# Four early expert slots instead of two, and slot 0's first product inside the last attention batch

## The chip, the cores and the metric

The kernel runs on one core of a Trainium2 chip. The core has a matrix engine (PE, with its weight loads shown as PEld), a vector engine (DVE), a scalar engine (ACT), a general engine (POOL), and a queue engine (SP) that here only issues transfers. Each engine executes its own instructions strictly in the order in which the program gives them; semaphores hold it where it needs another's result. The metric is the device time of one execution in microseconds (us), lower is better.

## The reference

Attention over 4 batches of 8 heads, 768 positions and 64 channels, in blocks of 32 keys: every query sees its neighbours within 16 positions and one summary (maximum of k, mean of v) of each block. Its output, 3072 tokens of 512 channels, goes through a mixture of 8 experts, of which each token uses the one with the largest logit:

```python
scores_l_m = np.where(mask_l, scale * (q @ k.T), -1e9)      # |i - j| < 16
scores_s = scale * (q @ k_sum.T) + np.log(32)               # k_sum: max over 32 keys
a = softmax(concat(scores_l_m, scores_s)); x = a @ concat(v, v_sum)
e_idx = argmax(x @ w_gate); gate = softmax(x @ w_gate)[e_idx]
eom = sigmoid(x @ w_output_gate)
for e in range(8):
    out[mask_e] = gate * eom[:, e] * (relu(x[mask_e] @ w1[e]) @ w2[e])
```

w1 of an expert is 512 x 1024, w2 is 1024 x 512. All inputs and the output are float32.

## The kernel before

*Attention.* `attention` (line 169) goes through 48 stages: batch, token tile of 128 (`tok`, 6 in a batch), and half of the heads (`g`). A stage multiplies queries and keys (`scores`), takes exponentials on ACT (`pr`), transposes them on PE (`turn_p`), and multiplies by values (`values`), whose result `xs` is written to `x_dr` in DRAM. Beside that run the loads and transposes of later batches. Value blocks lie in a ring of `VR` = 9 tiles (line 34), each loaded by SP when the block that used it before is done. After every two token tiles come the logits (`turn_x`, `logits`, `turn_logits`), and after every batch the routing (`route`, line 393): the position of each token in its expert's list is counted with matmuls, and six scatters on POOL write the token numbers and factors into `l_dr`. The last batch's last logits and its routing cannot come before its last stage.

*Experts.* The tokens of an expert are worked on in slots of 256. For a slot, POOL fetches its list (`fetch_list`, line 693, two indirect transfers), gathers its tokens from `x_dr` (`fetch`, line 707, two more), PE transposes them (`take_x`, into high and low parts `xh`, `xl`), the first product makes 8 hidden blocks (`first`, line 755: 12 matmuls of 256 columns each), and the second product (`second`, line 856: 8 blocks of 6 matmuls of 512 columns) makes the output, which `write` scatters on POOL. In the middle of a slot's second product stand the transposes of the next slot's tokens and the gather for the one after it. Weights come in tiles of 128 x 512 (`fetch_w`, line 716): SP loads a raw tile, ACT makes its high part (line 733), DVE its low part (line 734). Each of w1 and w2 has 8 tiles per expert, and only one set of them is kept, so a tile is loaded when the slot before is done with it. SP reads the expert's number from the slot's table first (`value_load`).

*Slots.* `EARLY` = 2 slots are taken from what the first two batches fill: `early_slots` counts full blocks of 256 per expert after these batches' routing. Their lists and slot 0's gather are issued in the last batch (event "routed", handled by `start`). All other slots come from `rest_slots` (line 633), after the last batch's routing: as many full ones as there are, then halves of 128. Slots 1 to 7 run in any case, further ones under nested conditions.

*The hand-over.* Slot 0's w1 is loaded in the stages of token tile 3 of the last batch and the first half of its w2 in those of tile 4 (lines 782 and 783). The second half of w2 lies where attention's tiles are, so it comes after them. `early` (line 785) puts slot 0's transposes and its first product behind the last stage, with the five pieces of the last routing between its blocks (`ROUTE_AT`); then come the rest of the weights, `rest_slots`, slot 2's list, and slot 0's second product.

*Order.* A planner simulates the program and fixes each engine's order from it; within `manual_schedule` an engine keeps the order in which the program is written (SP in attention; POOL, and DVE for some weights, behind it). `late_work` lists work that the last batch's stages take along.

Of the kernel before, what the change touches and what calls it, by code (L numbers as in the profile page):

```python
# [20 lines left out]
P = 128  # L21
# [28 lines left out]
EARLY = 2  # L50
REST = N - EARLY * SLOT

SURE = -(-(REST - E * SLOT // 2) // SLOT)
MOST = (REST + E * (SLOT // 2 - 1)) // SLOT
# [39 lines left out]
def body(tc, q, k, v, w_gate, w_ogate, w1, w2, ident, cst, out):  # L94
    nc = tc.nc
    with (
# [14 lines left out]
        l_dr = dr.tile([E * N, 2], I32, name="l_dr")  # L111
# [6 lines left out]
        late_work = [[] for _ in range(TB)]  # L118
# [27 lines left out]
def route_setup(tc, const, sa, ps, c_sb, l_dr):  # L146
# [15 lines left out]
    fill = sa.tile([P, E * N // P, 2], I32, name="fill")  # L162
    nc.gpsimd.memset(fill[:, :, 1:2], 0)
    nc.gpsimd.iota(fill[:, :, 0:1], pattern=[[1, E * N // P]], base=NOLIST, channel_multiplier=E * N // P)
# [4 lines left out]
def attention(tc, const, sa, sb, st, ps, dr, q, k, v, id_sb, c_sb, wg_sb, x_dr, l_dr, rt, late_work):  # L169
# [335 lines left out]
    for i, (b, tok, g) in enumerate(stages):  # L505
        u, tt = tok // 2, tok % 2
        n1, n2 = step_after(b, u), step_after(b, u, 2)
        more = b + 1 < B
        if (b, tok, g) == (B - 1, 0, 0):
# [50 lines left out]
        if b == B - 1 and i == n - 2 * TB + 5:  # L560
            yield "routed"
# [378 lines left out]
```

## Time and profile before

| What | Value |
|---|---|
| runs | 575.73, 562.63, 572.33 us; median 572.33 |
| the profiled execution | 563.66 us, span 561.8 us, mean clock 0.949 |
| PE busy | 500.7 us, 89% of the span, 3880 matmuls |
| DVE, ACT, POOL busy | 395.9 us (70%), 339.1 us (60%), 193.1 us (34%) |
| moved by DMA | 117.63 MB, mean 209 GB/s |
| first-product matmuls | 3 lines with 384 each, that is 12 full slots |

"Busy" is the share of the span in which an engine executes; PE's matmuls overlap, so a busy PE is not PE at its peak. The clock is the share of full speed that the chip granted to PE. A wait is put down to what ended it. Attention fills roughly the first 210 us, the full slots the time to about 500 us, the halves the rest.

### The profile page before, as it was taken

To read this page: it belongs to the slowest core of one execution; us is meant where nothing else is said; L and a number is where in the kernel's file an instruction comes from. 1 tells how busy PE (TensorE), PEld (TensorE's weight loads), DVE (VectorE), ACT (ScalarE), POOL (GpSimd) and SP (SyncE) were. 2 spreads that over 40 slices of the span, in tenths; PEclk is the share of its full clock that TensorE was granted. 3 is DMA by queue.
4 is the path that set the end of the run, shared out by engine and by line. 5 is a ranking of instruction groups with operands and counts; after the bars stand their busy time and mean duration, and the time that the engine had idled before them with its cause. 6 is when DMAs were issued, how large, how long until landed. Compare 5 with 4: busy or idle time off the path is not lost. (4 is left out here: it accounts for less than half of the span.)

```text
span 561.8 us, 12246 instructions
## 1 busy us (share of the span) xinstructions
PE 500.7 (89%) x3880; PEld 436.5 (78%) x3880; DVE 395.9 (70%) x1210; ACT 339.1 (60%) x752; POOL 193.1 (34%) x222
## 2 busy tenths in 40 slices
PE   6498998988979789985999999999999999987990
PEld 5497786767768678874989989899898998975770
DVE  8878798759838857952767665776656666666892
ACT  4386786675749747442656554665555655547881
POOL 6036145445541420337643625415113031130111
PEclk8599998998979979997999999999999999998996
DMA  9979999999764874159667485774856737439790
GB/s 233 232 186 251 235 241 250 115 219 232 163 138 120 247 253 150 65 162 317 211 225 272 151 282 185 236 277 139 300 181 232 269 128 264 168 114 332 252 322 26
DMA packets 116799, 117.63 MB, mean 209 GB/s; under 512 B 53598, under 2 KB 78462, under 8 KB 115952
## 3 DMA queue, kind: packets, MB, share of 16 engines
q1 hardware_dynamic: 107584, 97.02, 61.3%
q0 software_dynamic: 9136, 19.69, 11.5%
q8 instruction: 34, 0.56, 0.5%
q14 instruction: 45, 0.37, 0.2%
HBM read 105.50 MB, written 13.79 MB: 212 GB/s over the span
## 5 line engine op out<-in xcount | busy, mean ns | idle before, releaser
L764 PE MATMUL hp<-xhl,w1h 128*128 128x256 f32 x384 | 109.0, 285 | 0.0
L765 PE MATMUL hp<-xhl,w1l 128*128 128x256 f32 x384 | 108.8, 284 | 0.0
L763 PE MATMUL hp<-xhl,w1h 128*128 128x256 f32 x384 | 108.4, 286 | 0.0
L733 ACT ACTIVATE w2h<-raw 128x512 fp32r<-128x512 f32 x104 | 64.7, 629 | 60.5 <-PE yp L854 27.7
L734 DVE TENSOR_TENSOR w2l<-raw,w2h 128x512 fp32r<-128x512 f32 x104 | 70.5, 689 | 35.2 <-ACT w2h L733 34.2
L852 PE MATMUL yp<-w2h,hh 128*128 128x512 f32 x216 | 87.3, 404 | 0.1
L853 PE MATMUL yp<-w2l,hh 128*128 128x512 f32 x216 | 85.4, 395 | 0.0
L854 PE MATMUL yp<-w2h,hl 128*128 128x512 f32 x216 | 85.2, 396 | 0.1
L331 ACT ACTIVATE pr<-sm,mn 128x120 f32<-128x120 f32 x192 | 62.1, 387 | 26.1 <-DVE mn L329 25.8
L763 PEld LDWEIGHTS hp<-xhl,w1h 128*128 128x128 f32 x384 | 73.7, 193 | 2.0 <-DVE w1l L734 0.4
L712 POOL DMA_INDIRECT xg<-x_dr,lst x28 | 32.3, 1152 | 124.5 <-PE xp L745 106.1
L764 PEld LDWEIGHTS hp<-xhl,w1h 128*128 128x128 f32 x384 | 74.1, 193 | 1.2 <-DVE xhl L748 0.2
L765 PEld LDWEIGHTS hp<-xhl,w1l 128*128 128x128 f32 x384 | 74.1, 193 | 0.0
L766 ACT ACTIVATE hh<-hp 128x256 fp32r<-128x256 f32 x96 | 36.5, 381 | 59.1 <-PE hp L765 57.0
L734 DVE TENSOR_TENSOR w1l<-raw,w1h 128x512 fp32r<-128x512 f32 x104 | 66.2, 690 | 7.3 <-ACT w1h L733 6.2
L767 DVE SCALAR_TENSOR_TENSOR hl<-hp,hh 128x256 fp32r<-128x256 f32 x96 | 39.6, 421 | 44.8 <-ACT hh L766 44.7
L321 PE MATMUL sp<-kt,qt 128*128 128x120 f32 x384 | 58.7, 301 | 7.9 <-DVE kt L296 7.0
L733 ACT ACTIVATE w1h<-raw 128x512 fp32r<-128x512 f32 x104 | 58.2, 621 | 6.9 <-DMA raw<-in_moe_w_dram 6.5
L321 PEld LDWEIGHTS sp<-kt,qt 128*128 128x128 f32 x384 | 53.8, 215 | 10.4 <-issue 8.3
L329 DVE CUSTOM_DVE_ANT_0 sm<-sp,c_sb 128x120 f32<-128x120 f32 x192 | 42.9, 277 | 14.6 <-PE sp L321 13.1
L854 PEld LDWEIGHTS yp<-w2h,hl 128*128 128x128 f32 x216 | 40.7, 189 | 9.5 <-DVE hl L823 0.5
L852 PEld LDWEIGHTS yp<-w2h,hh 128*128 128x128 f32 x216 | 41.2, 191 | 8.6 <-ACT hh L822 0.5
(285 smaller groups left out, 906.5 us busy)
## 6 DMA issues: line engine op xcount, KB each, us to landing
raw<-in_moe_w_dram SPq DMA_DIRECT2D x208, 256.0 KB
vw<-in_v_dram SPq DMA_DIRECT2D x88, 96.0 KB
raw_k<-in_k_dram SPq DMA_DIRECT2D x12, 512.0 KB
raw_q<-in_q_dram SPq DMA_DIRECT2D x12, 512.0 KB
vm<-in_v_dram SPq DMA_DIRECT2D x8, 768.0 KB
x_dr<-xs POOLq DMA_DIRECT2D x24, 256.0 KB, 5.8
vw<-vs_dr SPq DMA_DIRECT2D x36, 48.0 KB
vw<-in_v_dram SPq DMA_DIRECT2D x8, 64.0 KB
```

What stands on the lines that cost most here:

```text
L321: nc.tensor.matmul(sp[:, 2 * x + y, 0:W], lhsT=qt[:, 2 * g + x, li, :], rhs=kt[:, 2 * g + x, blk * KW:blk * KW + W], start=True, stop=True)
L329: nc.vector.tensor_tensor_reduce(out=sm[:, c, :], in0=sp[:, c, 0:W], in1=c_sb[:, m:m + W], scale=1.0, scalar=3.0e38, op0=ALU.add, op1=ALU. ...
L331: nc.scalar.activation(pr[:, c, :], sm[:, c, :], AF.Exp, bias=mn[:, c:c + 1], scale=-1.0)
L733: nc.scalar.activation(hi, raw, AF.Copy)
L734: nc.vector.tensor_tensor(lo, raw, hi.bitcast(F32), ALU.subtract)
L763: nc.tensor.matmul(hp, lhsT=w_h[:, fs], rhs=self.xh[:, c, :], start=c == 0, stop=False)
L764: nc.tensor.matmul(hp, lhsT=w_h[:, fs], rhs=self.xl[:, c, :], start=False, stop=False)
L765: nc.tensor.matmul(hp, lhsT=w_l[:, fs], rhs=self.xh[:, c, :], start=False, stop=c == NC - 1)
L767: nc.vector.scalar_tensor_tensor(hl[:, j, :], hp, 0.0, hh[:, j, :].bitcast(F32), ALU.max, ALU.subtract)
L852: nc.tensor.matmul(y, lhsT=hh[:, j, tk], rhs=w_h, start=j == 0, stop=False)
L853: nc.tensor.matmul(y, lhsT=hh[:, j, tk], rhs=w_l, start=False, stop=False)
L854: nc.tensor.matmul(y, lhsT=hl[:, j, tk], rhs=w_h, start=False, stop=j == NF - 1)
```

## The change

`EARLY` becomes 4, and the event "routed" comes in stage 10 of batch 2 (`ROUTED_AT`); the lists of all four early slots are fetched there. Their gathers read only the rows of the first two batches. At the last batch's first stage slot 0's gather is issued and `late_work` is filled from a table, `LATE`, one entry per stage: "10" is tile 0 of w1, "x" slot 0's transposes with slot 1's gather behind them, "b0" block 0 of its first product, "20" tile 0 of w2. The blocks use the PSUM tag TR. After the last stage the second half of slot 0's w2 and all of slot 1's w1 are loaded, and `tail` executes slot 0's second product in a fixed order on PE, with the five pieces of the last routing ("r" in `TAIL`) between its blocks. Then come `rest_slots` and the other slots. Their lists are fetched from slot 2 on, six per slot (three before). An early slot that does not exist would get an empty list, for which `l_dr` has 128 more rows. The ring of value tiles has 8 instead of 9.

```diff
-VR = 9
+VR = 8
+ROUTED_AT = 10
-ROUTE_AT = (-1, 0, 1, 2, 4)
+LATE = ("10 11", "12 13", "14 15", "x 16", "17 b0", "b1 20", "b2 21", "b3 22", "b4 23", "b5 b6", "b7")
+TAIL = ("r", 0, "r", 1, "r", 2, 3, "r", "r", 4, 5, 6, 7)
+LISTS = 6
-EARLY = 2
+EARLY = 4
+FIRST = 2
...
-                if event == "last batch":
+                if event == "routed":
+                    moe.add_slots(early_slots(tc, const, c_sb, rt))
+                    for s in range(EARLY):
+                        moe.fetch_list(s, 2)
+                elif event == "last batch":
                     pool_a.__exit__(None, None, None)
                     moe.open_first(tc.tile_pool(name="moe1", bufs=2, side="left", reuse_waits="tile"))
-                elif event == "routed":
-                    moe.add_slots(early_slots(tc, const, c_sb, rt))
                     moe.start(late_work)
                 elif event[0] == "tiles done":
-                    moe.early(event[1])
+                    route = event[1]
...
+        with tc.manual_schedule(engines={mybir.EngineType.DVE}):
+            moe.fetch_w(2, 0, range(NF // 2, NF))
+            moe.fetch_w(1, 1, range(NF))
+        moe.tail(route)
+        slots, halves, counts = rest_slots(tc, const, c_sb, rt)
+        moe.add_slots(slots)
+        halves = halves()
         with tc.manual_schedule(engines={mybir.EngineType.Pool}):
-            with tc.manual_schedule(engines={mybir.EngineType.DVE}):
-                moe.fetch_w(2, 0, range(NF // 2, NF))
-                moe.fetch_w(1, 1, range(NF // 2))
-                slots, halves, counts = rest_slots(tc, const, c_sb, rt)
-            moe.add_slots(slots)
-            moe.fetch_list(EARLY, 2)
-            moe.fetch_w(1, 1, range(NF // 2, NF))
-            moe.second(0, 2, *moe.hidden0, 1, 2, 2)
-            halves = halves()
             moe.run(halves)
...
+        if i == FIRST * 2 * TB + ROUTED_AT:
+            yield "routed"
...
-        if b == B - 1:
-            w = late_work[tok]
-            take = w[:-(-len(w) // 2)] if g == 0 else w[:]
-            del w[:len(take)]
-            second += take
+        if late_work:
+            second += late_work.pop(0)
...
-        rows = (B - 1) * S if s in range(EARLY) else N
+        rows = FIRST * S if s in range(EARLY) else N
...
     def start(self, late_work):
-        for s in range(EARLY):
-            self.fetch_list(s, 2)
         self.fetch(0, 2)
-        late_work[3] += [lambda: self.fetch_w(1, 0, range(NF))]
-        late_work[4] += [lambda: self.fetch_w(2, 0, range(NF // 2))]
-
-    def early(self, route):
-        self.take_x(2, "S")
-        self.fetch(1, 2)
         self.hidden0 = self.hidden()
-        for j in range(-1, NF):
-            if j >= 0:
-                self.first(j, self.hidden0, None, "S" if j % 2 else "PT")
-            if j in ROUTE_AT:
-                with self.tc.high_priority():
-                    route.pop(0)()
+        def work(what):
+            if what == "x":
+                self.take_x(2)
+                self.fetch(1, 2)
+            elif what[0] == "b":
+                self.first(int(what[1]), self.hidden0, None, "TR")
+            else:
+                self.fetch_w(int(what[0]), 0, [int(what[1])])
+        late_work += [[lambda x=x: work(x) for x in stage.split()] for stage in LATE]
+
+    def tail(self, route):
+        yp = self.accumulators(2)
+        with self.tc.manual_schedule(engines={mybir.EngineType.PE}):
+            for what in TAIL:
+                if what == "r":
+                    with self.tc.high_priority():
+                        route.pop(0)()
+                    continue
+                self.second_step(what, yp, *self.hidden0, 1, 2, 2)
+        self.write(0, yp)
...
-        later = [(s, 2) for s in range(EARLY + 1, EARLY + NITEM)] + [(("half", h), 1) for h in range(E)]
+        later = [(s, 2) for s in range(EARLY, EARLY + NITEM)] + [(("half", h), 1) for h in range(E)]
         for s in range(1, EARLY + SURE):
-            n = len(later) if s == EARLY + SURE - 1 else 3
+            n = len(later) if s == EARLY + SURE - 1 else 0 if s < EARLY - 2 else LISTS
```

`second_step` is one block of the second product with what `second` did around it (`take_x` and `fetch` ahead of block 4, the next slot's w2 tile behind each).

More of the change, by code (lines that the diff above doesn't have):

```diff
@@ L110, in body @@
         x_dr = dr.tile([N, DM], F32, name="x_dr")
-        l_dr = dr.tile([E * N, 2], I32, name="l_dr")
+        l_dr = dr.tile([E * N + P, 2], I32, name="l_dr")
         pool_a = tc.tile_pool(name="early", bufs=1, side="left")
@@ L565, in attention, with slot_tables @@
     b, tok = B - 1, TB - 1
-    rest = [lambda: values(n - 1), lambda: turn_x(b, tok), lambda: logits(b, tok),
-            lambda: (turn_logits(b, tok), route_to(b)), lambda: route_to(b)]
+    values(n - 1)
+    rest = [lambda: turn_x(b, tok), lambda: logits(b, tok), lambda: turn_logits(b, tok), lambda: route_to(b),
+            lambda: route_to(b)]
     yield "tiles done", rest
-def slot_tables(tc, const, c_sb, name, n, t, r):
+def slot_tables(tc, const, c_sb, name, n, t, r, empty=False):
     nc = tc.nc
@@ L660, in __init__ @@
         self.id_sb, self.x_dr, self.l_dr, self.rt, self.out = id_sb, x_dr, l_dr, rt, out
-        self.slots, self.expert = {}, {}
+        self.slots, self.expert, self.lists = {}, {}, {}
     def fixed(self, pool, name, n, shape, dt):
@@ L673, in open_first @@
         self.xg = self.fixed(self.mp, "xg", 2, [P, DM], F32)
-        self.lists = {}
         self.xh, self.xl = self.fixed(self.mp, "xhl", 2, [P, NC, SLOT], F32R)
@@ L854, in second_block, with accumulators, second_step @@
             nc.tensor.matmul(y, lhsT=hl[:, j, tk], rhs=w_h, start=False, stop=j == NF - 1)
+    def accumulators(self, n):
+        return [self.ps.tile([P, DM], F32, name=f"yp{t}", tag="PV", bufs=PB["PV"]) for t in range(n)]
+    def second_step(self, j, yp, hh, hl, nxt, nxt2, nxt_n):
+        if j == 4:
+            self.take_x(nxt_n)
+            self.fetch(nxt2, nxt_n)
+        self.second_block(j, yp, hh, hl)
+        self.fetch_w(2, nxt, [j])
     def second(self, s, n, hh, hl, nxt, nxt2, nxt_n):
-        yp = [self.ps.tile([P, DM], F32, name=f"yp{t}", tag="PV", bufs=PB["PV"]) for t in range(n)]
+        yp = self.accumulators(n)
         for j in range(NF):
-            if j == 4:
-                self.take_x(nxt_n)
-                self.fetch(nxt2, nxt_n)
-            self.second_block(j, yp, hh, hl)
-            self.fetch_w(2, nxt, [j])
+            self.second_step(j, yp, hh, hl, nxt, nxt2, nxt_n)
         self.write(s, yp)
```

24 lines of the change are left out of this document (13 added, 11 removed).

## The prediction

> **What bounds the kernel now.** I read the page first, then sums by stretch, then who waited for whom around the hand-over from attention to the experts, then PE, POOL and DVE in order of time there.
>
> ```profile
> span 561.8 us, 12246 instructions
> ```
> ```profile
> 167.00:192.00 25.00, 25.00 (x318) 21.75 (x315) 21.35 (x134) 23.24 (x61) 6.88 (x8) 1.00 0.64 174
> 192.00:205.00 13.00, 8.30 (x50) 6.22 (x50) 8.64 (x27) 6.60 (x16) 5.74 (x7) 0.74 0.57 162
> ...
> 251.00:267.00 16.00, 7.67 (x34) 6.32 (x34) 6.04 (x10) 5.39 (x11) 11.80 (x12) 0.79 0.94 313
> ```
>
> The columns of the stretches are: length, then busy time (with instructions) of PE, weight load, DVE, ACT and POOL, then granted clock, DMA share and GB/s. All of it is in the last batch of attention and just behind it. From 167 to 192 PE has no idle time (25.00 of 25). Then two holes follow: 192 to 205, and 251 to 267. Each costs its idle time, and what runs beside it runs at a lower clock. The first: 13.00 - 8.30 = 4.7 us idle, and 26% of 8.30 = 2.2 us lost to a clock of 0.74, together 6.9 us. The second: 8.3 us idle and 21% of 7.67 = 1.6 us, together 9.9 us. So 16.8 us are to be had here.
>
> What made the holes:
>
> ```profile
> PE xp L745 <- DMA xg<-x_dr,lst: 8.3, 1, 8.3
> ...
> ACT w2h L733 <- DMA raw<-in_moe_w_dram: 5.3, 3, 2.7
> ...
> PE pt L339 <- ACT pr L331: 4.7, 4, 2.9
> ```
> ```profile
> 205.40 0.28 PE L764 MATMUL hp<-xhl,w1h 128*128 128x256 f32 x1
> 205.52 0.28 PE L765 MATMUL hp<-xhl,w1l 128*128 128x256 f32 x1
> ...
> 250.41 0.39 PE L853 MATMUL yp<-w2l,hh 128*128 128x512 f32 x1
> 250.64 0.40 PE L854 MATMUL yp<-w2h,hl 128*128 128x512 f32 x1
> 259.38 0.66 PE L745 MATMUL xp<-id_sb,xg 128*128 128x128 f32 x2 [8.33 <-DMA xg<-x_dr,lst]
> ```
>
> In the waits the numbers are total, times and longest. The second hole is one wait: PE stands, in the middle of slot 1's second product, for the gathered tokens of slot 2. The first is four waits for exponentials on ACT, which itself stood for weight tiles (5.3 us) ahead of them in its queue. Matmuls of 256 columns start 0.12 us apart (205.40, 205.52), of 512 columns 0.23 us (250.41, 250.64).
>
> ```profile
> 158.91 0.99 POOL L699 DMA_INDIRECT lst<-l_dr,rowia  x1 [7.94 <-DVE xs L360]
> 160.21 0.96 POOL L699 DMA_INDIRECT lst<-l_dr,rowia  x1 [0.30 <-issue]
> ...
> 169.21 1.04 POOL L712 DMA_INDIRECT xg<-x_dr,lst  x1 [0.30 <-issue]
> ...
> 246.53 1.00 POOL L699 DMA_INDIRECT lst<-l_dr,rowib  x1 [5.75 <-issue]
> 247.83 0.97 POOL L699 DMA_INDIRECT lst<-l_dr,rowib  x1 [0.30 <-issue]
> 251.84 1.16 POOL L712 DMA_INDIRECT xg<-x_dr,lst  x1 [3.04 <-DMA lst<-l_dr,rowib]
> ```
>
> Slot 2 is the first that needs the routing of the last batch, so its list is fetched only at 246.53, after that batch's scatters, and its gather issues at 251.84. The lists of slots 0 and 1 came with the four transfers from 158.91 on.
>
> **The change part by part.** *Slots 2 and 3 taken early.* Counting the reference's routing, the first two batches give expert 2 596 tokens and expert 4 768, which is 2 + 3 full blocks of 256: four early slots exist and none is empty. The total stays at 12 full slots and 3 halves, as now, so the matmuls are the same. Slot 2's gather no longer waits for the last batch; it goes out in slot 0's second product, when its buffer is free. The first slot with a late list is slot 4, two slots later. The second hole goes: -9.9 us. What is late next is slot 4's list, which now stands behind two more slots of PE work (some 22 us each: 96 matmuls 0.12 us apart and 48 at 0.23 us), against a lateness of 8.3 us; it is covered.
>
> ```profile
> SPq L722 <- DVE counts L650: 17.7, 1, 17.7
> SPq L255 <- PE pt L339: 12.1, 1, 12.1
> ...
> SPq L731 <- ACT pr L331: 6.4, 1, 6.4
> ```
>
> SP also stood 17.7 us for slot 2's expert number, with slot 2's weights queued behind it. That wait moves to slot 4 too; it counts nothing, since the gather was later still.
>
> *Slot 0's first product moved into the last batch.* PE executes the same 96 matmuls (11.5 us) and 8 transposes, but ahead of the last stages' remnants instead of behind them. As PE is full from 167 on, moving work gains only what falls into holes: between 0 and -6.9 us. I take -6.9 here and list the new waits below. The reason: the loads of w1 now stand in SP's queue from the batch's first stages, before the 12.1 us for which SP stands at a value block, not after it; so most of ACT's 5.3 us for late weight tiles, the cause of the first hole, should go.
>
> ```profile
> L733 ACT ACTIVATE w1h<-raw 128x512 fp32r<-128x512 f32 x104 | 58.2, 621 | 6.9 <-DMA raw<-in_moe_w_dram 6.5
> ...
> L767 DVE SCALAR_TENSOR_TENSOR hl<-hp,hh 128x256 fp32r<-128x256 f32 x96 | 39.6, 421 | 44.8 <-ACT hh L766 44.7
> L766 ACT ACTIVATE hh<-hp 128x256 fp32r<-128x256 f32 x96 | 36.5, 381 | 59.1 <-PE hp L765 57.0
> ```
>
> ACT gets 8 x 0.381 = 3.0 us more in the stages, DVE 8 x 0.421 = 3.4 us; the 12 weight conversions and the evacuations of slot 0's tokens were in this stretch already. From 167 to 205 ACT was busy 29.84 of 38 us and DVE 29.99; with these 33, still below PE's 31 us of work there plus 9 us of first products that now come ahead. PE stays the bound, though ACT at 23.24 of 25 has little slack in single stages.
>
> *New waits, each from 0 up.* (a) Eight list transfers instead of four go out on POOL before slot 0's gather, 1.3 us apart (158.91 to 160.21), so the gather, last issued at 169.21, could be 5.2 us later; behind it on POOL stand the writes of x and, on PE, whatever is planned after slot 0's transposes. Its gather no longer waits for batch 2's rows, and the planner sees the same delay, so 0 to +5.2, taken 1. (b) ACT may still stand for a weight tile: 0 to +5.3 by the row above, taken 1, since seven of eight w1 loads get out before SP's long wait. (c) The eight blocks use the PSUM tag TR (2 buffers) with the attention's transposes and logits; the nearest row is a wait of 0.56 us that this tag caused, so 0 to 8 x 0.56 = 4.5, taken 1:
>
> ```profile
> 231.47 1.36 PE L745 MATMUL xp<-id_sb,xg 128*128 128x128 f32 x8 [0.56 <-DVE at L424]
> ```
>
> (d) The tail. The last routing no longer has 11.5 us of first product to hide it, only blocks of the second product, 6 x 0.23 = 1.4 us each.
>
> ```profile
> 209.98 0.42 DVE L360 TENSOR_TENSOR xs<-pv,den 128x256 f32<-128x256 f32 x1
> ...
> 214.62 0.69 DVE L734 TENSOR_TENSOR w2l<-raw,w2h 128x512 fp32r<-128x512 f32 x1 [0.23 <-ACT w2h L733]
> ...
> 224.63 0.18 DVE L188 COPY lg<-lt 128x32 f32<-128x32 f32 x1
> ...
> 227.68 0.19 DVE L414 CAST ohb<-oh 128x48 bf16<-128x48 f32 x1
> ```
>
> From the logits' copy to the one-hot cast DVE took 3.2 us (224.63 to 227.87), with four weight conversions between; PE's order is fixed there, and blocks 2 and 3 cover 2.8 us of that chain. With some wait before the copy and for the last xs, 0 to +5, taken 2. The second half of w2 lost its cover too: its load waits for the last exponential (SP's 6.4 us) and its last conversion ended 5.3 us after the last xs (209.98 to 215.31). Blocks 4 to 7, which read it, come after four blocks (5.6 us) and the routing steps, transposes included, so it is just covered: nothing.
>
> *The rest.* One value buffer fewer: each value load waits for a use one block later. SP's wait of 12.1 us came at the second load of a pair and now comes at the first; what stands behind it is the last w1 tile and w2, needed stages later, nothing. Four fewer small loads, one more table operation, eight more list transfers at about 1 us on POOL: POOL was busy 193 of 562 us, and 12 lists in a slot take 15.5 us, less than the 17 us before that slot's gather is asked for. Nothing.
>
> Sum: -9.9 - 6.9 + 1 + 1 + 1 + 2 = -11.8 us. The profiled execution took 563.66 us (span 561.8), so 551.9 us on its own time. The runs before were 575.73, 562.63 and 572.33; the profiled one lies near the fastest, 8.7 us under the median. I take the gain off the median: 572.3 - 11.8 = 560.5 us.
>
> One rule weighs on the small holes. The Trainium skill, page "TensorE: Matmul & The Clock Gate", section "Why this matters for your kernels", says that only idle gaps above about 3 us bring the clock back to half. The longest wait in the first hole was 2.9 us, yet the clock over those 13 us was 0.74, so here the trace does not agree. By the page the tail's waits of 1 to 2 us cost no more than themselves (560.5); by the trace a cluster of them could cost 2.2 us again (562.7).
>
> **The rivals.** *The fill is given back* (0.30). The gather's hole goes, but ACT, at 23.24 of 25 in the full stretch, delays the exponentials as much as before and PE finds no use for the moved blocks. For it: ACT is in order and gets 3 us more. Against: PE has 9 us more work than ACT's total. -9.9 + 5 = about -5, 567 us.
>
> *Nothing gained* (0.12). The gather of slot 0 is late by the whole 5.2 us of (a), the other new waits are as taken, and the fill is undone by it: -9.9 + 5.2 + 4 = -0.7, 572 us. For it: POOL is strictly in order, and the lists could not go before 158.91, when the scatters had landed. Against: the gather also loses its wait for batch 2.
>
> *Slower* (0.08). ACT, in its fixed order, stands at a weight conversion whose load stands in SP's queue behind a value load, which waits for PE. Its price is SP's 12.1 us, with some 2 us of clock; the fill is undone and the tail costs 2: -9.9 + 14.1 + 2 = +6, 578 us. Without the fill it decides from a wait of about 6 us (slower at all) and 17 us (over 2%). Against: the planner issues ACT's work by the same queue, and in the trace ACT's longest such wait there was 2.7 us.
>
> *The change does not do what it says*: early slots empty, so that extra passes run; the count above excludes it for these inputs.
>
> **How the numbers follow.** Forecast 0.50, rivals 0.30, 0.12, 0.08. The forecast's own range: best -16.8 (555.5), worst -7 (565). Runs of this kernel differ by 13 us, so the low end is the best case on a run some 6 us under the median, 549; the high end is the nothing-gained case, 572; beyond lie the slower case and part of the noise, 2 in 10. About 2% (11.4 us) is what a measurement of this kernel can tell from no change. The forecast lies just beyond it: of its 0.50 I count 0.44 as faster, of the first rival 0.06; same gets 0.06 + 0.24 + 0.11 + 0.03; slower 0.01 + 0.05.
>
> **What would show it.** In the profile after: no wait of PE for xg near the hand-over, and slot 2's transposes following slot 1's fourth block without a gap (else the first step is wrong). First-product matmuls before the last stage's transposes, and the clock at 1.00 from the last batch's middle on (else the fill is). Waits of PE in the tail for ls, ohb or w2l of 2 us in all; far more would mean that the cover was too thin. PE waiting for xg or ACT for raw inside the last batch would be (a) or (b). The number of first-product matmuls must stay 384 per line. The prediction is wrong if the stages of the last batch take over 13 us longer than now.

## The result and the profile after

| | before | after |
|---|---|---|
| runs beside each other | 575.73, 562.63, 572.33, 568.71 us; median 570.52 | 591.59, 600.23, 599.51, 599.37 us; median 599.44 |
| ratio | | 1.057 (95%: 1.043 to 1.071) |
| span of the profiled execution | 561.8 us | 589.6 us |

The kernel became 5.7% slower where 2% faster was forecast. The ratio compares fast executions alone (562.63 and 568.71 of the four before), since some executions of any kernel here fall into a slower state; the medians of all give 1.051. The profiled execution after is its fastest, so the trace shows 27.8 us of loss and the medians 28.9. The trace of before (563.66 us) is none of the four runs in the table, so it need not come from the chip of the trace after; that matters for the time ahead of the last batch.

The page after begins, and its sums by stretch are (columns as in the prediction):

```profile
span 589.6 us, 12261 instructions
```
```profile
163.60:186.00 22.40, 16.77 (x139) 14.57 (x138) 13.53 (x71) 15.37 (x39) 8.57 (x10) 0.85 0.50 152
186.00:204.00 18.00, 15.41 (x177) 13.44 (x176) 15.08 (x69) 12.60 (x32) 3.81 (x5) 0.91 0.69 204
204.00:225.40 21.40, 19.13 (x182) 16.56 (x182) 9.66 (x53) 9.14 (x25) 7.06 (x8) 0.84 0.49 125
225.40:252.20 26.80, 22.77 (x135) 18.25 (x134) 22.65 (x87) 14.54 (x28) 6.07 (x6) 0.87 0.56 186
252.20:275.60 23.40, 23.40 (x154) 21.39 (x153) 15.17 (x35) 12.72 (x27) 8.85 (x7) 1.00 0.72 226
275.60:301.20 25.60, 24.11 (x153) 21.23 (x152) 13.84 (x26) 13.00 (x27) 17.68 (x16) 1.00 0.64 208
301.20:328.70 27.50, 25.90 (x154) 22.41 (x153) 16.12 (x30) 13.89 (x28) 17.80 (x16) 0.94 0.57 188
328.70:362.40 33.70, 27.57 (x153) 23.90 (x152) 15.73 (x29) 13.28 (x27) 14.89 (x15) 0.85 0.49 162
362.40:387.60 25.20, 24.08 (x153) 21.39 (x153) 15.30 (x28) 13.40 (x27) 10.32 (x10) 1.00 0.62 202
387.60:411.00 23.40, 23.40 (x154) 21.37 (x153) 15.36 (x28) 13.51 (x27) 5.49 (x5) 1.00 0.66 226
```

The first four rows are the last batch and its end, the others one slot each, 1 to 6, from one first product to the next. Slot 1 takes 23.40 us with PE full, and so does slot 6. Slots 2 to 5, which are the same work, take 25.6, 27.5, 33.7 and 25.2; in the four of them POOL is busier than in slot 6. Slots 2 to 7 together, before and after:

```profile
266.60:407.40 140.80, 140.80 (x913) 127.92 (x912) 94.58 (x168) 82.37 (x166) 58.05 (x55) 1.00 0.68 227
```
```profile
275.60:434.40 158.80, 148.46 (x914) 131.69 (x913) 91.71 (x163) 80.59 (x162) 70.71 (x66) 0.96 0.60 199
```

The same matmuls, 18.0 us more, 10.3 of them idle on PE. Three markers divide the rest: the last batch's first scores begin at 154.0 us before and 163.6 after (+9.6); from there to slot 2's first product it is 112.6 and 112.0 (-0.6, where the prediction had -11.8); slots 2 to 7 +18.0; behind them +0.8. Together 27.8.

What happens in slot 4, in order of time, on POOL:

```profile
331.27 1.03 POOL L899 DMA_INDIRECT out_dram<-y,lst  x1 [3.89 <-DVE hl L777]
332.61 1.00 POOL L899 DMA_INDIRECT out_dram<-y,lst  x1 [0.31 <-issue]
333.92 1.00 POOL L709 DMA_INDIRECT lst<-l_dr,rowib  x1 [0.30 <-issue]
335.22 1.02 POOL L709 DMA_INDIRECT lst<-l_dr,rowib  x1 [0.30 <-issue]
```

then on PE:

```profile
340.34 0.28 PE L773 MATMUL hp<-xhl,w1h 128*128 128x256 f32 x1
340.46 0.28 PE L774 MATMUL hp<-xhl,w1h 128*128 128x256 f32 x1
340.58 0.28 PE L775 MATMUL hp<-xhl,w1l 128*128 128x256 f32 x1
341.26 0.38 PE L773 MATMUL hp<-xhl,w1h 128*128 128x256 f32 x1 [0.41 <-issue]
341.99 0.28 PE L774 MATMUL hp<-xhl,w1h 128*128 128x256 f32 x1 [0.35 <-issue]
342.69 0.37 PE L775 MATMUL hp<-xhl,w1l 128*128 128x256 f32 x1 [0.43 <-issue]
344.81 0.37 PE L773 MATMUL hp<-xhl,w1h 128*128 128x256 f32 x1 [1.74 <-issue]
```

and the waits of all engines from 340 to 350 us:

```profile
ACT hh L776 <- remote: 10.9, 1, 10.9
...
PE hp L773 <- issue: 2.5, 3, 1.7
...
POOL lst L709 <- issue: 1.8, 6, 0.3
```

Until 340.58 PE's matmuls start 0.12 us apart, then 0.7 us and more. No semaphore that the profile shows holds them: their releaser is "issue". ACT gets nothing done for 10.9 us. Only POOL goes on at its pace, a transfer by an index every 1.3 us with 0.3 us between: this is the run of two writes of the output and eleven list transfers (to 347.56) that `LISTS` = 6 makes at the start of this slot. The crawl begins 9.3 us after the run's first transfer and ends about 2 us after its last; from 349.70 on matmuls start close together again (349.70, 349.88, 350.10).

Theory 1 is that these runs of list transfers stall the other engines. Its rivals were the instruction order, the weight loads, and, for the 9.6 us ahead of the last batch, the smaller value ring.

### The profile page after: what moved, and what is told of

Its sections match the earlier page's. It is cut to its first block, busy times and chain, and to the rows that moved or that the text cites. A ratio compares the mean times of both kernels' runs of the same rounds, so it can differ in the third digit from the quotient of the medians.

```text
span 589.6 us, 12261 instructions
## 1 busy us (share of the span) xinstructions
PE 514.2 (87%) x3880; PEld 445.4 (76%) x3880; DVE 389.6 (66%) x1211; ACT 337.8 (57%) x752; POOL 204.1 (35%) x228
## 3 DMA queue, kind: packets, MB, share of 16 engines
q0 software_dynamic: 9392, 19.70, 10.5%
## 4 chain that ended last, share of the span: by engine, by line
PE 54%; issue 14%; DMA 14%; DVE 7%; ACT 3%; SPq 2%; POOL 2%; another core or an unknown queue 2%; POOLq 0%; ACTq 0%; DVEq 0%
PE hp L773 8%; PE hp L775 7%; PE hp L774 7%; PE yp L871 7%; PE yp L872 7%; PE yp L870 7%; DMA vm<-in_v_dram 4%; DMA raw_q<-in_q_dram 4%; PE sp L329 3%; DMA raw_k<-in_k_dram 2%; PE pv L358 2%; PE xp L755 2%; DMA xg<-x_dr,lst_half 2%; DMA raw<-in_moe_w_dram 2%
## 5 line engine op out<-in xcount | busy, mean ns | idle before, releaser
L773 PE MATMUL hp<-xhl,w1h 128*128 128x256 f32 x384 | 110.9, 289 | 3.0 <-issue 2.5
L774 PE MATMUL hp<-xhl,w1h 128*128 128x256 f32 x384 | 109.9, 286 | 2.2 <-issue 2.2
L775 PE MATMUL hp<-xhl,w1l 128*128 128x256 f32 x384 | 110.1, 287 | 1.9 <-issue 1.9
L871 PE MATMUL yp<-w2l,hh 128*128 128x512 f32 x216 | 87.0, 403 | 1.7 <-issue 1.7
L872 PE MATMUL yp<-w2h,hl 128*128 128x512 f32 x216 | 87.2, 404 | 0.8 <-issue 0.7
L773 PEld LDWEIGHTS hp<-xhl,w1h 128*128 128x128 f32 x384 | 74.7, 195 | 4.3 <-issue 2.2
L774 PEld LDWEIGHTS hp<-xhl,w1h 128*128 128x128 f32 x384 | 74.9, 195 | 3.2 <-issue 2.3
L329 PE MATMUL sp<-kt,qt 128*128 128x120 f32 x384 | 56.9, 297 | 7.3 <-DVE kt L304 7.1
L329 PEld LDWEIGHTS sp<-kt,qt 128*128 128x128 f32 x384 | 52.6, 211 | 9.7 <-issue 8.5
L872 PEld LDWEIGHTS yp<-w2h,hl 128*128 128x128 f32 x216 | 42.0, 194 | 12.8 <-issue 3.1
L871 PEld LDWEIGHTS yp<-w2l,hh 128*128 128x128 f32 x216 | 42.1, 195 | 10.4 <-issue 2.8
```

Of the source, the lines that this page charges most:

```text
L329: nc.tensor.matmul(sp[:, 2 * x + y, 0:W], lhsT=qt[:, 2 * g + x, li, :], rhs=kt[:, 2 * g + x, blk * KW:blk * KW + W], start=True, stop=True)
L773: nc.tensor.matmul(hp, lhsT=w_h[:, fs], rhs=self.xh[:, c, :], start=c == 0, stop=False)
L774: nc.tensor.matmul(hp, lhsT=w_h[:, fs], rhs=self.xl[:, c, :], start=False, stop=False)
L775: nc.tensor.matmul(hp, lhsT=w_l[:, fs], rhs=self.xh[:, c, :], start=False, stop=c == NC - 1)
L871: nc.tensor.matmul(y, lhsT=hh[:, j, tk], rhs=w_l, start=False, stop=False)
L872: nc.tensor.matmul(y, lhsT=hl[:, j, tk], rhs=w_h, start=False, stop=j == NF - 1)
```

## The experiments

All runs in one table, for reference below. "Before" is the kernel before on the same chip in the same group of runs; groups 2 to 6 fell on five different chips. Medians are over all executions, ratios as in the result. The last three columns come from each run's trace (for the kernel before, the one of 563.66 us): when the last batch's first scores begin, the time from there to slot 2's first product, and slots 2 to 7.

| run (group) | median, us | before | ratio (95%) | last batch at | to slot 2 | slots 2-7 |
|---|---|---|---|---|---|---|
| the kernel before (1) | 570.5 | | | 154.0 | 112.6 | 140.8 |
| the changed kernel (1) | 599.4 | 570.5 | 1.057 (1.043-1.071) | 163.6 | 112.0 | 158.8 |
| after_lists3 (2) | 582.8 | 567.6 | 1.0285 (1.023-1.034) | 159.9 | 111.1 | 155.2 |
| before_lists6 (2) | 593.1 | 567.6 | none given | 156.7 | 108.1 | 162.8 |
| before_vr8 (2) | 567.0 | 567.6 | 1.0019 (0.998-1.006) | 161.6 | 105.6 | 144.9 |
| after_vr9 (2) | 600.6 | 567.6 | 1.0595 (1.053-1.066) | 157.7 | 114.2 | 170.5 |
| before_early4 (3) | 565.8 | 560.2 | 1.0087 (1.005-1.013) | 153.0 | 104.0 | 151.4 |
| after_even_lists (3) | 554.5 | 560.2 | 0.9898 (0.985-0.995) | 153.3 | 104.7 | 140.0 |
| after_even_late_rank (3) | 550.8 | 560.2 | 0.9836 (0.978-0.989) | 154.0 | 98.5 | 141.0 |
| after_even_no_stage (3) | 559.4 | 560.2 | 0.9975 (0.993-1.002) | 154.6 | 110.5 | 140.3 |
| after_again (4) | 604.8 | 568.6 | 1.0676 (1.061-1.075) | - | - | - |
| after_even_again (4) | 590.9 | 568.6 | 1.0433 (1.038-1.049) | 165.1 | 111.3 | 161.5 |
| after_split_lists (4) | 601.5 | 568.6 | 1.0645 (1.058-1.071) | 162.0 | 116.4 | 166.5 |
| after_even_plain (4) | 588.6 | 568.6 | 1.0426 (1.037-1.049) | 160.6 | 112.3 | 163.1 |
| late_rank_again (5) | 547.7 | 558.9 | 0.9824 (0.977-0.988) | 152.6 | 97.7 | 140.7 |
| lists_behind_gather (5) | 550.4 | 558.9 | 0.9856 (0.980-0.991) | 154.7 | 96.1 | 140.5 |
| before_lists_behind (5) | 558.4 | 558.9 | 0.9980 (0.994-1.002) | 152.0 | 110.1 | 140.8 |
| early_lists_apart (5) | 547.5 | 558.9 | 0.9820 (0.977-0.987) | 152.2 | 97.3 | 140.9 |
| after_third (6) | 606.3 | 568.9 | 1.0710 (1.066-1.076) | 164.2 | 107.1 | 174.3 |
| early_lists_apart_again (6) | 574.0 | 568.9 | 1.0143 (1.009-1.020) | 161.1 | 106.0 | 146.6 |

The kernel before takes 567 to 571 us on the chips of groups 1, 2, 4 and 6, and 559 to 560 us on those of 3 and 5. I call them the slower and the quicker chips; each chip was met in one group only, so its part cannot be told from that of the time at which the group ran. No median of one sort is compared with one of the other except through the ratio.

**Fewer lists in the changed kernel.** One line:

```diff
-LISTS = 6
+LISTS = 3
```

> The changed kernel with three lists a slot in place of six. Theory 1: the 18 us that the steps of slots 2 to 5 are longer than 23.4 us (25.6, 27.5, 33.7 and 25.2 us) come from GpSimd's bursts of 12 list transfers, 16 to 20 us long with the writes of the output before them; with bursts of 6 each of these steps takes 23.4 to 24 us, and the kernel some 14 to 18 us less than the changed one, 580 to 586 us, with its span 571 to 576. What is left over, 12 transfers, comes in one burst in slot 7 and may cost up to 4 us there. Rival: the steps are long for another reason (the instruction order of the new program, the weight loads), and stay as long: within 3 us of the changed kernel.

Its slots 2 to 6 take 23.3 to 25.0 us each, and slot 7, in which the rest of the lists come as one run of 14 transfers, 33.9. The ratio falls from 1.057 to 1.0285; after_vr9 below, with six lists on the same chip, took 600.6 us, 17.8 more. Theory 1 holds, and the 10.5 us in a slot that had none of this loss before show that the loss moves with the lists.

**More lists in the kernel before.**

```diff
-            n = len(later) if s == EARLY + SURE - 1 else 3
+            n = len(later) if s == EARLY + SURE - 1 else 6
```

> The kernel before with six lists a slot in place of three, nothing else. Theory 1: bursts of 12 transfers slow TensorE here too: slots 1 to 4 together take 10 to 20 us more, the kernel 580 to 590 us. Rival: within 3 us of before.

The runs lie far apart; the lower two, 582.94 and 588.40 us, are 15 and 21 us above the median of before. In the trace (582.94) slots 2 to 7 take 22 us more than in the trace of before:

```profile
264.80:427.60 162.80, 149.39 (x914) 132.07 (x913) 94.30 (x168) 81.70 (x166) 57.08 (x55) 0.95 0.58 197
```

So the loss needs nothing else of the change. It lies in slots 2 and 3 (40.9 and 28.0 us), into which the longer runs fall; from slot 4 on each takes 23.5 us.

**The value ring,** alone in either kernel:

```diff
-VR = 9
+VR = 8
```
```diff
-VR = 8
-VP = 72
+VR = 9
+VP = 68
```

> The kernel before with a ring of eight value tiles in place of nine, nothing else. Theory 2: the 9.5 us that the changed kernel is late when the last batch's first scores begin (163.6 against 154.0 us) come from the ring: a load waits for the token before last instead of the one before that, and stands ahead of the other loads in SP's queue. Then this kernel loses 7 to 10 us, 577 to 581 us, and its last batch begins at 161 to 164 us. Rival: the 9.5 us come from the early lists and tables in the third batch or from another order of the vector work; then it is within 2 us of before.

> The changed kernel with nine value tiles, each row 68 and not 72 elements long so that they fit. Theory 2: 7 to 10 us less than the changed kernel, 589 to 592 us, with the last batch beginning at 154 to 156 us of the span. Rival: within 2 us of the changed kernel.

Neither moves the time: 1.0019 for the one, and the other, at 1.0595, stays where the changed kernel is. Theory 2 falls for the time. The kernel before with a ring of eight does begin its last batch late, at 161.6 us, and makes that up afterwards; what the four traces of this group say of that marker stands in the part on the prediction.

**Four early slots alone.** In the kernel before, with the ring of eight that it needs to fit; the tables' handling of empty slots comes with it. The kernel before takes its early slots from the first three batches (`rows = (B - 1) * S` in its `fetch`), not from two as said above, and this run keeps that.

```diff
-EARLY = 2
+EARLY = 4
...
-    slots, inc, exc = slot_tables(tc, const, c_sb, "a", EARLY, t, base)
+    slots, inc, exc = slot_tables(tc, const, c_sb, "a", EARLY, t, base, True)
```

> The kernel before with four early slots in place of two (from what three batches fill, as before; ring of eight so that it fits), and nothing else of the change: slot 0's first product, the order of the end of the last batch and three lists a slot stay. My theory: slot 2's wait (33.8 us for slot 1's step against 23.5) goes, 8 to 10 us less than before, ratio 0.982 to 0.986. Rival: the four more list transfers hold slot 0's gather back by as much, ratio 0.995 to 1.005.

My theory falls: 0.9% slower. PE still stands for gathers, now of slots 2 and 3 in turn:

```profile
PE xp L749 <- DMA xg<-x_dr,lst: 12.7, 3, 5.5
```

POOL's order shows why:

```profile
243.71 1.00 POOL L703 DMA_INDIRECT lst<-l_dr,rowib  x1 [9.43 <-DVE hsb L611]
245.01 1.23 POOL L703 DMA_INDIRECT lst<-l_dr,rowib  x1 [0.30 <-DVE hl L771]
246.55 1.55 POOL L716 DMA_INDIRECT xg<-x_dr,lst  x1 [0.30 <-PE yp L858]
```

Slot 2's gather no longer needs the last routing, but slot 4's list, which does, stands ahead of it in the order written out for POOL, and three more lists stand ahead of slot 3's. By this reading, what removed the wait in the changed kernel is the four slots together with the late lists' move behind slot 1.

**Even lists.** The changed kernel with 7 list transfers in each of slots 2 to 7 (three full slots and one half).

```diff
-        later = [(s, 2) for s in range(EARLY, EARLY + NITEM)] + [(("half", h), 1) for h in range(E)]
+        later = [(s, 2) for s in range(EARLY, EARLY + NITEM)]
+        single = [(("half", h), 1) for h in range(E)]
...
+            now = later[:n] + (single if last else single[:1] if n else [])
```

> The changed kernel with three lists of full slots and one of a half slot in each of slots 2 to 7: bursts of seven transfers, none of twelve. Theory 1: all steps of slots 2 to 10 take 23.3 to 25 us, 571 to 576 us, the 10 us of slot 7's burst in the run with three lists saved. What then remains over the kernel before is the last batch and its end. Rival: slot 7's 33.9 us step came from the branch that follows it and stays.

Better than expected: 1.0% faster than the kernel before, and slots 2 to 7 without any idle time on PE:

```profile
258.00:398.00 140.00, 140.00 (x913) 128.13 (x912) 91.75 (x163) 80.85 (x162) 67.66 (x66) 1.00 0.66 224
```

**The end of the last batch,** with even lists; of the two routing steps behind block 3 the last one moves behind block 6:

```diff
-TAIL = ("r", 0, "r", 1, "r", 2, 3, "r", "r", 4, 5, 6, 7)
+TAIL = ("r", 0, "r", 1, "r", 2, 3, "r", 4, 5, 6, "r", 7)
```

> The run with even lists, and TensorE's order at the end changed: the last two routing steps stand behind the second product's blocks 3 and 6 instead of both behind block 3. Theory 3: TensorE's 2.85 us wait for the expert index and the cold clock behind it go, 2 to 5 us less than with even lists. Rival: the vector engine is the bound there and the time comes back before slot 1 or in slot 2, within 1 us.

3.7 us less by the medians; the intervals of the two ratios overlap (0.985-0.995 and 0.978-0.989), but the time to slot 2 falls from 104.7 to 98.5 us, and group 5 gave 0.9824 again. In the order of the change PE stood for the expert index with four blocks of the second product behind it; from the waits of after_even_lists around that place:

```profile
PE rk L425 <- DVE ohb L422: 3.0, 1, 3.0
```

**The first product out of the stages,** with even lists:

```diff
-LATE = ("10 11", "12 13", "14 15", "x 16", "17 b0", "b1 20", "b2 21", "b3 22", "b4 23", "b5 b6", "b7")
-TAIL = ("r", 0, "r", 1, "r", 2, 3, "r", "r", 4, 5, 6, 7)
+LATE = ("10 11", "12 13", "14 15", "x 16", "17", "20", "21", "22", "23")
+TAIL = ("r", "b0", "r", "b1", "r", "b2", "r", "b3", "b4", "r", "b5", "b6", "b7", 0, 1, 2, 3, 4, 5, 6, 7)
```

> The run with even lists, but slot 0's first product (blocks b0 to b7) taken out of the last batch's stages and put between the routing steps behind them; x, the weights and the four early slots stay where the change put them. Theory 4: the blocks in the stages cost as much as they fill, so that this is within 3 us of the run with even lists or faster. Rival, my prediction: they fill 7 us of TensorE's idle time, so that without them the kernel takes 5 to 8 us more.

4.9 us more by the medians (the ratios' intervals, 0.993-1.002 and 0.985-0.995, just overlap) and 5.8 us later at slot 2. But the edit does more than move the blocks. The program loads slot 1's w1 ahead of `tail`, into the tiles that slot 0's w1 lies in, so the blocks in `tail` now wait for that second load and work with it (by the count in the prediction, slots 0 and 1 belong to the same expert). TensorE's waits from 205 to 245 us:

```profile
PE hp L773 <- ACT w1h L743: 7.2, 3, 5.5
```

That wait, of which even lists has nothing, is longer than the whole loss. So this run does not show that the blocks fill idle time, and theory 4 stays open.

**The same on another chip.** Since group 3 fell on a quicker chip, the changed kernel and even lists went again side by side, with two variants.

> The changed kernel itself, beside its variants on one chip, since the kernel before took 567.6 us in one group of runs and 560.2 in the other. Theory 1: the bursts of twelve are the larger part of the loss; it stands 18 to 40 us above the run with even lists, and the steps of slots 2 to 5 sum to 15 to 30 us over 4 x 23.3. Rival: the chip made the difference between 599 and 554 us; here it is within 12 us of the run with even lists.

> The run with even lists once more, for the comparison on one chip. Theory 1: ratio to before 0.985 to 0.995 again, steps of slots 2 to 10 between 23.3 and 24 us.

The result lies between the two. The change from twelve to seven transfers is worth 13.8 us here, less than theory 1 said; and even lists, without any loss in group 3, take 21.5 us more in slots 2 to 7:

```profile
276.40:437.90 161.50, 150.42 (x914) 132.46 (x913) 91.91 (x163) 81.15 (x162) 67.49 (x66) 0.96 0.59 194
```

So the same program on the same data crawls on one chip and does not on another. The issue of one slot's 16 weight loads on SP shows it as well, after_even_lists first, then after_even_again:

```profile
287.50 9.97 SPq L741 DMA_DIRECT2D raw<-in_moe_w_dram  x16
```
```profile
308.43 13.09 SPq L741 DMA_DIRECT2D raw<-in_moe_w_dram  x16
```

Two rivals can be looked up in these traces. Full DMA engines: in the stretches around these loads (281 to 300 and 302 to 325 us) the hardware queue kept the 16 engines busy for 55.9% on the quicker chip and for 54.3% on the slower one. Instruction loading: its queues moved one and two transfers there. Neither differs by much.

**Split, and plain.** In the changed kernel three of the six lists go behind the slot's gather; and in the run with even lists ten plain transfers of the same size, which nothing reads, follow each slot's lists.

```diff
-            for x in later[:n]:
+            for x in later[:(n + 1) // 2]:
                 self.fetch_list(*x)
+            self.behind = later[(n + 1) // 2:n]
```
```diff
+        for t in range(n):
+            i = nc.gpsimd.dma_start(got[:, t, :], self.l_dr[t * P:(t + 1) * P, :])
```

> The changed kernel with six lists a slot, but the last three of them behind that slot's gather, so that twelve transfers come as two bursts of six some 10 us apart. Theory 1a: it is the unbroken length that stalls the other engines; the steps take 23.3 to 25 us and the kernel is within 4 us of the run with even lists. Theory 1b: it is the number of transfers in a slot; the steps stay 2 to 10 us too long, within 6 us of the changed kernel.

> The run with even lists, and behind each slot's seven list transfers ten plain transfers of the same 1 KB from GpSimd's queue, into tiles that nothing reads: an unbroken run of 17 transfers and the output's two. Theory 1c: only transfers by an index stall the others; the steps stay at 23.3 to 24 us, within 2 us of the run with even lists. Theory 1d: any long run of GpSimd's transfers does; the steps of slots 2 to 7 take 26 to 34 us, 15 to 50 us more.

Splitting brings 3 us and leaves 166.5 us for the six slots, theory 1b by the numbers. But it tells little: in the first two of these slots the gather, the second half of the lists, the writes of the output and the next slot's lists came as one run of 16 transfers, so the run was not shortened. The plain transfers are clear: 588.6 against 590.9 us, and the six slots at 163.1 against 161.5, with POOL in its run for 5.4 us longer in each:

```profile
336.86 0.95 POOL L709 DMA_INDIRECT lst_half<-l_dr,rowic  x1 [0.30 <-issue]
337.81 5.43 POOL L722 DMA_DIRECT2D got<-l_dr  x10
```

This speaks for theory 1c: it is the transfers by an index that stall the others, not any transfer of GpSimd.

**Lists where SyncE is idle.** Even lists and the late rank once more, and beside it all lists behind the gather (six transfers in each of slots 1 to 7), the same move in the kernel before, and the early lists taken apart.

```diff
             self.fetch(nxt2, nxt_n)
+            for x in self.behind:
+                self.fetch_list(*x)
+            self.behind = []
```
```diff
-                    for s in range(EARLY):
-                        moe.fetch_list(s, 2)
+                    moe.fetch_list(0, 2)
...
-LATE = ("10 11", "12 13", "14 15", "x 16", "17 b0", "b1 20", "b2 21", "b3 22", "b4 23", "b5 b6", "b7")
+LATE = ("10 11", "12 13 l1", "14 15", "x 16", "17 b0", "b1 20 l2", "b2 21", "b3 22 l3", "b4 23", "b5 b6", "b7")
```

> Even lists and the late rank once more, beside the next three on one chip. If the chip is like the one of the third group (even lists 591 us, steps of 26 to 27.5), it takes 585 to 590 us; if like that of the second (554 us, steps of 23.3), 548 to 553.

> Late rank, and all list transfers (six in each of slots 1 to 7) moved from the start of a slot to behind its gather, when SyncE has issued the slot's weight loads. Theory 1e: the engines crawl only while SyncE issues weight loads and GpSimd runs transfers by an index; the steps of slots 2 to 7 take 23.3 to 24 us on any chip, and on a chip with long steps the kernel takes 15 to 25 us less than the run before it. Rival 1f: the burst alone does it, wherever it stands; the steps stay at 25 to 27.5 us, within 6 us. On a chip without long steps both are within 2 us.

> The kernel before, its three lists a slot moved behind the slot's gather (two before slot 1 starts, since the gathers need them). Theory 1e: on a chip with long steps 3 to 8 us less than the kernel before, on one without within 3 us of it. Rival: the wait for slot 3's gather grows, 2 to 8 us more.

> The run with lists behind the gather, and the four early lists taken apart: slot 0's where it was, slots 1 to 3's in the last batch's second, sixth and eighth stage. Theory 1: the burst of eight lists and a gather at the end of the third batch stalls the engines too (TensorE stood 4.2 us there with even lists on the chip with long steps and 0.8 us on the other); 4 to 9 us less on a chip with long steps, within 3 us on the other. Rival: that time was DMA-bound and nothing is gained, within 2 us.

This group fell on a quicker chip. There nothing stalls (140.5 to 140.9 us for the six slots in all four), so the positions make no difference and theories 1e and 1f stay untested by it. The changed kernel with short runs and the late rank is 1.4 to 1.8% faster than before there.

**The last pair,** the changed kernel and early_lists_apart on one chip:

> The changed kernel once more, to see it on a further chip. On a chip on which the kernel before takes 566 to 570 us: 599 to 606 us again, steps of slots 2 to 5 too long by 20 to 36 us together. On one on which the kernel before takes 557 to 562 us: theory 1, that bursts stall the engines only on the other chips, expects 552 to 556 us and steps of 23.3 us, so that the change is about 1% faster there; the rival, that twelve transfers in a burst stall on every chip, expects 565 us or more.

> Short bursts everywhere, beside the changed kernel. On a chip on which the kernel before takes 566 to 570 us, theory 1e (the engines crawl only while SyncE issues weight loads and GpSimd runs transfers by an index) expects steps of 23.3 to 24.5 us and 550 to 560 us, below the kernel before; rival 1f (the burst alone) expects steps of 25 to 27.5 us and 575 to 590 us. On the other kind of chip 546 to 550 us as before, which tells nothing of the two.

A slower chip again. The changed kernel loses 7.1%, its six slots 174.3 us; with short runs, moved lists and the late rank it loses 1.4%, its six slots 146.6 us:

```profile
271.30:445.60 174.30, 156.17 (x914) 135.67 (x914) 92.57 (x163) 81.23 (x162) 67.77 (x66) 0.91 0.55 180
```
```profile
267.10:413.70 146.60, 143.16 (x915) 129.03 (x914) 90.94 (x165) 78.57 (x162) 67.25 (x61) 1.00 0.62 217
```

32 of the 37 us by which the changed kernel stands above before are gone, and 28 of the 33.5 us of loss in the slots. The steps of slots 2 to 7 (23.3 to 25.3 us) are nearly what theory 1e expected, but the kernel's 574 us is far above 1e's 550 to 560 and 1 us below 1f's range. Slot 1 takes 28.6 us (24.7 on the quicker chip): TensorE's waits for "issue" there fall from 250.26 to 253.85, beside the six scatters of the last routing and the two writes of the output around them (242.34 to 252.40); slot 1's lists begin only at 265.81. From slot 1 on, gather, lists and writes come as unbroken runs of 10, one longer than the runs of 9 that cost 2.5 to 4.2 us in group 4; here slots 2 to 7 lose 0 to 2 us, so the number of transfers alone does not make the loss. But the lists in a run are six, not seven, and the chip is another. Whether the position makes the difference, and whether the stall needs SyncE's weight loads beside it, stays open. So does how the changed kernel itself, with its runs of twelve, does on a quicker chip: it only met slower ones.

## Why the prediction was wrong

The step that failed stands in the part on the rest: "eight more list transfers at about 1 us on POOL: POOL was busy 193 of 562 us, and 12 lists in a slot take 15.5 us, less than the 17 us before that slot's gather is asked for. Nothing." The arithmetic was right for POOL: the gathers were not late. What it left out is what a run of such transfers does to the engines beside it. Slots 2 to 7 became 18.0 us longer in group 1 and 33.5 in group 6 (174.3 less the 140.8 of the trace of before); putting six lists a slot into the kernel before cost at least 15 us, thinning them out brought 13.8 (group 4) and 17.8 (group 2). How the run slows the others stays open. The trace of before could not tell: its longest run, 20 transfers from 251.84 to 278.19 with the lists six and six in it, left slot 2 at 23.4 us. Nor does anything else in that trace stall as on the slower chips: between 25 and 500 us no wait of PE, ACT or DVE over 0.8 us ends with "issue" or "remote", while before_vr8, on the chip of group 2, has ACT stand 4.9 us so at 303 us, beside a run of eight. But a doubled run was then given as nothing, without the bounds that every other unknown got, and the range ended at 572.

The other steps:

- Slot 2's wait, -9.9 us: right. Slot 1's step fell from 33.8 to 23.4 us, in group 5 from 33.5 (before_lists_behind) to 24.7, and no wait for gathered tokens is left there. But the reason given was half of it; by the order in before_early4, the late lists had to leave POOL's queue ahead of slots 2 and 3 too. "What is late next is slot 4's list ... it is covered" held because of that.
- The filled hole, -6.9 with +3 for the waits (a) to (c): not shown. From the last batch's first scores to slot 1's first product PE has the same work in the variants compared here. In group 3 that takes 73.1 us in before_early4, 81.4 with even lists and 75.2 with the late rank; in group 5 it takes 76.5 in before_lists_behind and 74.3 with the late rank (the late rank's figures hold the 1.3 us of routing that it moves into slot 1). With the tail, the prediction has -1.9 for this stretch; the change's own order came out some 8 us longer, the late rank 2.1 longer and 2.2 shorter. So the rival "the fill is given back" is not excluded. Wait (a) was larger than the 1 us taken: PE stood 4.0 us for slot 0's tokens with even lists and 3.5 with the late rank.
- The tail (d), +2 in a range of 0 to 5: too small. Moving the last routing step behind three more blocks brought slot 2 forward by 6.2 us and the kernel by 3.7; the wait for the expert index alone was 2.9 us in group 1, and the four blocks that could have covered it stood behind it. The clock was 0.87 from 225.4 to 252.2 there (the fourth row of the first table of sums), against 1.00 from 205 to 260 with the late rank: the prediction's second figure, 562.7, had allowed for such a loss.
- The value ring, nothing: right for the whole time (1.0019).
- The time ahead of the last batch, priced at nothing: +9.6 us between the two traces, but not shown to be the change's. Group 2 has four traces on one chip: with a ring of nine the last batch begins at 156.7 us (before_lists6) and 157.7 (after_vr9), with a ring of eight at 161.6 (before_vr8) and 159.9 (after_lists3). So the ring moves it by 2 to 5 us there and the rest of the change by less than 2, either way. On the quicker chips it begins at 152.0 to 154.7 us in all eight traces, of either kernel. On the slower ones the kernel before has the same stalls: its first routing's six scatters come from about 96.5 to 104 us, and beside them ACT stood 5.7 us in before_lists6, which up to there is the kernel before. The same instruction in before_lists6, then in the trace of before:

```profile
105.02 0.60 ACT L192 ACTIVATE xT<-xtr 128x512 f32<-128x512 f32 x1 [5.69 <-remote]
```
```profile
100.97 0.60 ACT L192 ACTIVATE xT<-xtr 128x512 f32<-128x512 f32 x1 [1.23 <-PE xtr L369]
```

The trace of before, without such stalls, looks like those of the quicker chips, so much of the 9.6 us may be a difference of chips. The run of eight early lists and a gather adds to it: beside it ACT stood 9.9 us for "issue" in after_even_again, and in group 6 taking those lists apart brought the marker from 164.2 to 161.1.

```profile
ACT qt L200 <- issue: 9.9, 1, 9.9
```

On the chip of group 2 the hand-over gains nothing: slot 2 begins at 264.8 and 267.2 us in two variants of the kernel before, and at 271.0 and 271.9 in two of the changed one.

Where nothing stalls, the change with short runs is 5.8 us faster (even lists), and with the late rank as well 9.4 and 11.2 us faster (groups 3 and 5), against 11.8 predicted. That this comes near the sum is partly luck: these variants have another order of lists and tail than the change, and in group 5 slot 1's step alone, 33.5 to 24.7 us, is 8.8 of the 11.2. How the changed kernel itself does there is not known. The rival that ended slower was a wait of ACT behind SP's queue; the slower case came beside transfers on an engine that the stalled matmuls' waits do not name.

## What to carry to other kernels

Work that is off the critical path can still slow the other engines: give added transfers by an index a price on the other engines too, keep them in short runs, and look for matmuls that wait for "issue" beside them. Where an order is written out for a queue, a step that lost its dependence still waits for what stands ahead of it. And a variant that wins on one chip is to be tried on a second before it is believed: here one program went from 0.9898 to 1.0433.

## What the runs showed of the hardware

- Beside a run of transfers by an index on GpSimd, TensorE and ScalarE crawled in four of the six groups of runs, and SyncE's issue of 16 weight loads took 13.1 us instead of 10.0 in group 4. In group 6 the run in slot 3 began at 305.97 us and PE's matmuls, 0.12 us apart until 315.37, next started at 316.13, 316.35 and 317.56: some 9.5 us after the run's start, as in group 1. Runs of 8 transfers, two writes of the output and six lists, cost a slot 0 to 2 us on the slower chips (once 3.7, in group 6), runs of 9 (seven lists) cost 2.5 to 4.2, runs of 13 and 14 mostly 8 to 11 (2.3 and 4.1 in two slots of group 1). Runs of 10 cost 0 to 2 us in group 6, where they hold two gathers and six lists, and 4.5 in before_lists6, where they hold eight lists; so the number alone does not decide.
- The Trainium skill, page "DMA: Bandwidth & Descriptors", section "Anatomy of one DMA — SWDGE (gpsimd) path", says that a lot of descriptors can be emitted before the incremental cost shows up. On POOL itself the traces agree: in the longest runs one list still follows the other after about 1.26 us. The loss measured here is on the other engines.
- Groups 3 and 5 showed none of it with runs of 9 (six slots in 140.0 us) and of 10 (140.5). What sets these chips apart, the runs do not tell.
